# Small remainders of the experts' tokens as segments of one shared tile, in column tiles of TensorE

## The chip, the cores and the metric

The kernel runs on one core of a Trainium2 chip. The metric is the device time of one execution in microseconds (us). The kernel before takes 458.48 us, the median of three runs (458.1 to 458.9).

## The reference: what is computed

An attention block of the RWKV kind gives 3072 rows of 384 numbers; a mixture of eight experts with top-1 routing follows. The attention is not touched by the change and is left out here.

```python
# x: (N, D) = (3072, 384) from the attention; E = 8 experts, F = 1024
logits = x @ w_gate
expert_idx = np.argmax(logits, axis=1)
...                                            # gate_w: the softmax weight of the chosen expert
for e in range(E):
    mask = expert_idx == e
    xe = x[mask]
    h = np.maximum(xe @ w1[e], 0.0)            # (n_e, 384) @ (384, 1024)
    ye = h @ w2[e]                             # (n_e, 1024) @ (1024, 384)
    out[mask] = gate_w[mask, None] * ye
```

The inputs come from a fixed seed, so the number of tokens of each expert is known: 380, 348, 359, 410, 409, 389, 374 and 403. A kernel that works in tiles of 128 tokens of one expert needs 3, 3, 3, 4, 4, 4, 3 and 4 tiles for them, 28 in all. What goes beyond the last multiple of 128 is 124, 92, 103, 26, 25, 5, 118 and 19 tokens: four of the eight remainders are at most 32.

## The kernel before

The first stage (in the trace until about 138 us) is the attention in 32 units, with routing counts beside it; the second is the experts. Each of the 24 groups of 128 rows gets its logits and its expert; VectorE then works out which tile and which row of it each token takes (`ranks`, `bases`, `slots`, `index`), and which expert owns each tile (`owners`). A tile gathers its 128 rows from HBM with an indirect DMA, and scatters its results with another. All data are float32, apart from the one-hot matrices of the routing.

```python
C = 128; NG = N // C                           # 24
NTILE = NG + E - 1                             # 31: the most tiles that routing can need
NSURE = NG + E // 2                            # 28: run in any case
NEARLY = 2                                     # of these, run with tokens of the first half only, early

class Tile:
    def load_w1(self, wp, part=0):             # w1 of the tile's expert, 1536 KB, two buffers
        ...
            e = self.expert(ENG.SP)            # a register, from self.R.ei
            nc.sync.dma_start(self.w1, w1[ds(e, 1)].rearrange("a p d f -> p (a d) f"))

    def turn(self, mo, tag, copy=nc.vector.tensor_copy):
        p = self.R.ps.tile([128, DT, 128], FP32, name="xTp", tag=tag, bufs=BUFS[tag])
        for d in range(DT):                    # DT = 3
            nc.tensor.transpose(p[:, d, :], self.xs[:, 128 * d:128 * d + 128], ident)
        self.xT = self.tile(mo, [128, DT, 128], "xT", 2)
        copy(self.xT, p)

    def hidden(self, mo, fb):                  # fb 0 and 1: half of F each
        ...
        p = self.R.ps.tile([128, 4, 128], FP32, name="hp", tag=f"P{fb}", bufs=2)
        for f in range(4):
            o = (4 * fb + f) * 128
            for d in range(DT):
                nc.tensor.matmul(p[:, f, :], lhsT=self.w1[:, d, o:o + 128], rhs=self.xT[:, d, :],
                                 start=d == 0, stop=d == DT - 1)
        nc.scalar.activation(self.hT[:, 4 * fb:4 * fb + 4, :], p, func=ACT.Relu)

    def result(self, mo):
        p = self.R.ps.tile([128, DM], FP32, name="yp", tag="y", bufs=2)
        e = slice(self.j, self.j + 1) if self.early else ds(self.expert(ENG.PE), 1)
        for f in range(FT):                    # FT = 8; w2 of all experts is resident
            rhs = w2_all[:, e, f * DM:(f + 1) * DM]
            nc.tensor.matmul(p, lhsT=self.hT[:, f, :], rhs=rhs, start=f == 0, stop=f == FT - 1)
        self.y = self.tile(mo, [128, DM], "yo", 3)
        nc.vector.tensor_scalar_mul(self.y, p, self.xs[:, DM:W])

def run_tiles(tiles, wp, mo):                  # called with tiles 2 to 27
    for j, t in enumerate(tiles):
        if j + 2 < len(tiles):
            tiles[j + 2].load_x(mo)
        t.hidden(mo, 0)
        t.hidden(mo, 1)
        if j + 2 < len(tiles):
            tiles[j + 2].load_w1(wp)
        if j + 1 < len(tiles):
            tiles[j + 1].turn(mo, "g")
        t.result(mo)
        t.store()
```

Between the attention and this loop stand two early tiles and the last of the routing (cut to the order of the steps):

```python
t0.hidden(mo, 0); ...                          # routing of the last 6 groups
w2_load(NW); w2_load(NW + 1)                   # 1536 KB each, on SyncE's queue
...
t0.hidden(mo, 1); t1.turn(la, "g", nc.scalar.copy)
R.bases(rt); R.slots(rt); ...; R.owners(rt)    # VectorE
t2.load_w1(wp)                                 # needs owners
t0.result(mo)
R.index(rt, "rw")                              # TensorE and VectorE: the row numbers to gather
t2.load_x(mo); t3.load_x(mo); t0.store()
for e in range(NW + 2, E): w2_load(e)          # the last two
t1.hidden(mo, 0); t1.hidden(mo, 1); t3.load_w1(wp)
t1.result(mo); t1.store(); t2.turn(mo, "g")
late = late_rows(R, NSURE - NEARLY, rt)        # gathers rows for tiles that may not be needed
run_tiles(tiles[2:], wp, mo)
late_tiles(R, NSURE - NEARLY, late)            # under a condition; not taken with these inputs
```

One part of the attention matters for reading the trace: its outputs are written by matmuls that use only half of the array's columns each, so that `hi` = 0 and `hi` = 1 go to different partitions of one PSUM tile.

```python
def u_out(u):
    ...
    yp = ps.tile([128, HC, C], FP32, name="yp", tag="y", bufs=2)
    for c in range(HC):
        ...
        for hi in range(2):
            q = slice(64 * hi, 64 * hi + 64)
            if old is not None:
                nc.tensor.matmul(yp[q, c, :], lhsT=old[:, hi, :], rhs=x["R"][:, c, :],
                                 start=True, stop=False, skip_group_check=True)
        for hi in range(2):
            q = slice(64 * hi, 64 * hi + 64)
            nc.tensor.matmul(yp[q, c, :], lhsT=vh(x, c, hi, 64), rhs=x["A"][:, hi, c, :],
                             start=old is None, stop=True, skip_group_check=True)
```

Of the kernel before, what the change touches and what calls it, by code (L numbers as in the profile page):

```python
# [9 lines left out]
FP32 = mybir.dt.float32  # L10
# [9 lines left out]
E, F = 8, 1024  # L20
# [12 lines left out]
NTILE = NG + E - 1  # L33
NSURE = NG + E // 2
# [12 lines left out]
def rwkv5_then_switch(ctx, tc, r, k, v, rk, tok, wu_in, wl, wg, wgh, w1, w2, out):  # L47

# [345 lines left out]
    def fast():  # L394
# [220 lines left out]
        with tc.manual_schedule():  # L615
# [19 lines left out]
            for u in range(NU):  # L635
                if u + 4 < NU:
                    u_load(u + 4)
                if HP <= u < HP + 4 * NW:
                    w2_load((u - HP) // 4, u % 4, 4)
                elif HP + 4 * NW <= u < HP + 4 * NW + NEARLY * DT:  # L640
                    tiles[(u - HP - 4 * NW) // DT].load_w1(wp, (u - HP - 4 * NW) % DT)
                if u + 2 < NU:
                    u_scale(u + 2)
                    u_scale_g(u + 2)
                if u + 1 < NU:
                    if u:
                        u_scores(u + 1)
                    u_state(u + 1)
                    u_mask(u + 1)
                u_out(u)  # L650
                if u == 2:
                    R.begin()
                    gate_weights()
                if u >= HP and u % HP < HC:
                    u_gate(u // HP - 1, u % HP, "rw")
                for step in todo[u]:
                    step()
                for j in range(NEARLY):
                    if u == NU - HP:
                        tiles[j].load_x(la)  # L660
# [20 lines left out]
            R.bases(rt)  # L681
            R.slots(rt)
# [5 lines left out]
            R.owners(rt)  # L688
            t2.load_w1(wp)
            t0.result(mo)  # L690
            R.index(rt, "rw")
# [5 lines left out]
            t1.hidden(mo, 0)  # L697
# [5 lines left out]
            late = late_rows(R, NSURE - NEARLY, rt)  # L703
            run_tiles(tiles[2:], wp, mo)
        em.close()
        late_tiles(R, NSURE - NEARLY, late)
# [3 lines left out]
    class Routes:  # L710
# [5 lines left out]
        def __init__(self, ps, la, na):  # L716
            self.ps, self.na = ps, na
            self.run = la.tile([128, B + 1, E], FP32, name="run")
            self.rl = la.tile([128, 2, NG], FP32, name="rl")
            self.At = la.tile([128, NG, 128], BF16, name="At")  # L720
            self.la = la
            self.pad = [la.tile([128, E + E // 2], FP32, name=f"pad{i}") for i in range(4)]
            if na:
                self.full = la.tile([128, na], FP32, name="full")
                self.isA = la.tile([128, NG], FP32, name="isA")
# [103 lines left out]
        def bases(self, rt):  # L829

            na = self.na
            ci = rt.tile([128, E], I32, name="ci")
            nc.vector.tensor_scalar_add(ci, self.run[:, B], 127.0)
# [3 lines left out]
            nc.vector.tensor_copy(til[:, z], ci)  # L837
            if na:
                nc.vector.tensor_tensor(til[:, E // 2:E // 2 + na], til[:, E // 2:E // 2 + na], self.full,
                                        op=ALU.subtract)  # L840
            for i in range(3):
                t = self.pad[i + 1]
                nc.vector.tensor_tensor(t[:, z], last[:, z], last[:, E // 2 - (1 << i):E + E // 2 - (1 << i)],
                                        op=ALU.add)
                last = t
            self.last = last[:, z]
            self.base = rt.tile([128, E], FP32, name="base")
            nc.vector.tensor_tensor(self.base, self.last, til[:, z], op=ALU.subtract)
# [3 lines left out]
        def owners(self, rt):  # L852

            tge = rt.tile([1, NTILE, E], FP32, name="tge")
            nc.vector.tensor_tensor(tge, bc(iota_f[0:1, 0:NTILE, None], [1, NTILE, E]),
                                    bc(self.last[0:1, None, :], [1, NTILE, E]), op=ALU.is_ge)
            ef = rt.tile([1, NTILE], FP32, name="ef")
            nc.vector.tensor_reduce(ef, tge, axis=AX, op=ALU.add)
            self.ei = rt.tile([1, NTILE], I32, name="ei")
            nc.vector.tensor_scalar_min(self.ei, ef, float(E - 1))  # L860
            self.nt = rt.tile([1, 1], I32, name="nt")
            nc.vector.tensor_copy(self.nt, self.last[0:1, E - 1:E])

        def slots(self, rt):
# [6 lines left out]
            if self.na:  # L871
                nc.vector.scalar_tensor_tensor(out=jt, in0=self.isA, scalar=-1000.0, in1=jt, op0=ALU.mult, op1=ALU.add)
            Bm = rt.tile([128, NG, NTILE], BF16, name="Bm")
            nc.vector.tensor_tensor(Bm, bc(iota_f[:, None, 0:NTILE], [128, NG, NTILE]),
                                    bc(jt[:, :, None], [128, NG, NTILE]), op=ALU.is_equal)
            self.Bv = rt.tile([128, NG, 2, NTILE], BF16, name="Bv")
            nc.scalar.activation(self.Bv[:, :, 1, :], Bm, func=ACT.Copy, scale=lo_f)
            nc.vector.tensor_tensor(self.Bv[:, :, 0, :], Bm, bc(hi_b[:, :, None], [128, NG, NTILE]), op=ALU.mult)

        def index(self, rt, tag):  # L880
            self.idx = self.to_index(rt, self.Bv, NTILE, NG, tag, "idx")

    class Tile:
# [8 lines left out]
        def load_w1(self, wp, part=0):  # L892
            j, R = self.j, self.R
            if part == 0:
                self.w1 = self.tile(wp, [128, DT, F], "w1s", 2)
            if self.early:
                nc.sync.dma_start(self.w1[:, part], w1[j, :, part])
            else:
                e = self.expert(ENG.SP)
                nc.sync.dma_start(self.w1, w1[ds(e, 1)].rearrange("a p d f -> p (a d) f"))  # L900

        def expert(self, eng):
            return nc.values_load(self.R.ei[0:1, self.j:self.j + 1], engines=[eng], min_val=0, max_val=E - 1,
# [24 lines left out]
        def hidden(self, mo, fb):  # L928
# [5 lines left out]
            for f in range(4):  # L934
                o = (4 * fb + f) * 128
                for d in range(DT):
                    nc.tensor.matmul(p[:, f, :], lhsT=self.w1[:, d, o:o + 128], rhs=self.xT[:, d, :],  # L937
# [19 lines left out]
    def run_tiles(tiles, wp, mo):  # L957

        for j, t in enumerate(tiles):
            if j + 2 < len(tiles):  # L960
                tiles[j + 2].load_x(mo)
            t.hidden(mo, 0)
            t.hidden(mo, 1)
            if j + 2 < len(tiles):
                tiles[j + 2].load_w1(wp)
            if j + 1 < len(tiles):
                tiles[j + 1].turn(mo, "g")
            t.result(mo)
            t.store()

    def late_rows(R, first, pool):

        xs = pool.tile([128, NTILE - first, W], FP32, name="xl")
        late = [Tile(R, j, late=True) for j in range(first, NTILE)]
        for i, t in enumerate(late):
            t.load_x(xs[:, i])
        return late

    def late_tiles(R, first, tiles):

        count = nc.values_load(R.nt[0:1, 0:1], min_val=0, max_val=NTILE,
                               skip_runtime_bounds_check_because="at most NTILE tiles by their count")
        with tc.If(count > first):
            with tc.tile_pool(name="lt", bufs=1) as lt:
                with tc.manual_schedule():
                    for t in tiles:
                        t.load_w1(lt)
                        t.turn(lt, "g")
                        t.hidden(lt, 0)
                        t.hidden(lt, 1)  # L990
# [3 lines left out]
    def after_general():  # L994
# [10 lines left out]
        R.owners(rt)  # L1005
# [3 lines left out]
        with tc.manual_schedule():  # L1009
# [4 lines left out]
            late = late_rows(R, NSURE, rt)  # L1014
            run_tiles(tiles, mo, mo)
        em.close()
        late_tiles(R, NSURE, late)
# [15 lines left out]
def _layout(name, *a):  # L1033
# [26 lines left out]
    elif name == 'moe_w1':  # L1060
        a = a.reshape(E, DT, 128, F).transpose(0, 2, 1, 3)
# [24 lines left out]
```

## Time and profile before

| what | value |
|---|---|
| time, median of 3 runs | 458.48 us |
| span of the profiled execution | 456.2 us |
| TensorE matmul, busy | 439.0 us (96% of the span) |
| TensorE weight load, busy | 368.0 us (81%) |
| VectorE, ScalarE, GpSimd, busy | 147.1, 129.2, 158.2 us |
| moved by DMA | 95.45 MB, mean 209 GB/s |
| w1 loads of a tile in the loop | 26, 1536 KB each, 6.7 us to landing |

Busy times are sums of the records of an engine; records of one engine overlap on TensorE, because its matmuls are pipelined, so the start-to-start distance of its records tells more than their length. A float32 matmul of this program leaves two records: 48 of them are the 24 matmuls of one tile's two `hidden` calls, 16 are the eight of its `result`. In the rows of the chain of waits, the first number is the start of a step, the second its length, both in us. In the timeline, a row is one group of like instructions that follow one another: start, length, engine, line, operation, tiles, shapes, count. An array use is given as rows*columns (128*64 is half the columns).

### The profile page before, as it was taken

The page shows a single profiled execution, that of the slowest core. Times are in us where ns is not written, and L with a number is a line of the kernel's source. Part 1 is how long each engine was busy: PE and PEld are TensorE (multiplying, and loading weights), DVE is VectorE, ACT ScalarE, POOL GpSimd, SP SyncE. Part 2 cuts the span into 40 slices and gives each one's busy share as a digit, 9 for nine tenths or more (in the row PEclk, how much of TensorE's full clock was granted, in tenths as well). Part 3 has the DMA queues.
Part 4 walks back from the last instruction along what each step waited for, and adds up shares of the span by engine and source line. Part 5 has one row for each costly group of instructions (what it writes and reads, how often), then busy time and mean ns, then how long its engine had stood idle before and what let it go on. Part 6 is the DMA issues. An engine that isn't in the chain of part 4 may idle for free.

```text
span 456.2 us, 10424 instructions
## 1 busy us (share of the span) xinstructions
PE 439.0 (96%) x4176; PEld 368.0 (81%) x4176; DVE 147.1 (32%) x394; ACT 129.2 (28%) x390; POOL 158.2 (35%) x192
## 2 busy tenths in 40 slices
PE   7899998998999988999999999999999999999993
PEld 7799997997999876887777777778888888888871
DVE  6576785996896401111111111111111111111100
ACT  3777775775773101111111111111111111111110
POOL 6997747946840243111111111111122221111000
PEclk9999998998999999999999999999999999999999
DMA  7488859869743999644555555555544544555400
GB/s 274 127 262 287 301 163 374 337 194 376 301 140 118 394 415 285 243 172 169 185 181 191 190 199 190 175 192 177 174 159 174 180 167 175 180 183 174 157 19 13
DMA packets 24576, 95.45 MB, mean 209 GB/s; under 512 B 3840, under 2 KB 6950, under 8 KB 20676
## 3 DMA queue, kind: packets, MB, share of 16 engines
q1 hardware_dynamic: 20322, 83.40, 51.2%
q0 software_dynamic: 3904, 11.23, 8.3%
q8 instruction: 38, 0.62, 0.5%
q14 instruction: 22, 0.18, 0.1%
q10 hardware_dynamic: 290, 0.02, 0.0%
HBM read 85.18 MB, written 10.24 MB: 209 GB/s over the span
## 4 chain that ended last, share of the span: by engine, by line
PE 51%; issue 36%; POOL 6%; DMA 2%; another core or an unknown queue 1%; DVE 1%; ACT 1%; POOLq 0%; SPq 0%; ACTq 0%; DVEq 0%
PE hp L937 13%; PE yp L946 12%; PE P L497 5%; PE yp L558 5%; PE P L487 5%; PE yp L554 4%; PE rp L587 4%; POOL xs L918 3%; PE Gp L533 2%; DMA w_all<-in_r_k_units_dram 2%; POOL out_dram L951 2%; PE xTp L924 1%; PE warm L444 1%; POOL w_all L467 0%
## 5 line engine op out<-in xcount | busy, mean ns | idle before, releaser
L937 PEld LDWEIGHTS hp<-xT,w1s 128*128 128x128 f32 x1344 | 154.3, 192 | 7.8 <-DVE xT L926 1.1
L937 PE MATMUL hp<-xT,w1s 128*128 128x128 f32 x1344 | 155.1, 275 | 0.8 <-DVE xT L926 0.8
L946 PE MATMUL yp<-w_all,hT 128*128 (+1 forms) x448 | 149.5, 487 | 1.6 <-ACT hT L939 1.2
L946 PEld LDWEIGHTS yp<-w_all,hT 128*128 128x128 f32 x448 | 82.9, 190 | 54.1 <-ACT hT L939 1.8
L939 ACT ACTIVATE hT<-hp 128x512 f32<-128x512 f32 x56 | 33.4, 597 | 265.5 <-PE hp L937 252.3
L951 POOL DMA_INDIRECT out_dram<-yo,idx x26 | 26.5, 1018 | 221.7 <-DVE yo L948 212.2
L508 ACT ACTIVATE A<-ident,dv 128x128 f32<-128x128 f32 x192 | 59.6, 389 | 0.2 <-ACT dv L505 0.2
L926 DVE COPY xT<-xTp 128x384 f32<-128x384 f32 x27 | 15.1, 557 | 132.2 <-PE xTp L924 122.4
L948 DVE TENSOR_SCALAR yo<-yp,xs 128x384 f32<-128x384 f32 x26 | 16.1, 618 | 123.4 <-PE yp L946 123.4
L466 POOL TENSOR_TENSOR w_all<-w_all 128x384 f32<-128x384 f32 x31 | 34.8, 1123 | 27.2 <-DMA w_all<-in_r_k_units_dram 9.9
L558 PE MATMUL yp<-A,w_all 128*64 128x128 f32 x384 | 40.5, 282 | 0.1
L519 DVE COPY_PREDICATED A<-mask,P 128x384 f32<-128x384 int32 x64 | 33.8, 583 | 9.6 <-ACT A L508 9.4
L918 POOL DMA_INDIRECT xs<-x_hbm,idx x26 | 25.3, 974 | 29.8 <-PE hp L937 22.5
L554 PE MATMUL yp<-w_all,St 128*64 128x128 f32 x320 | 33.5, 282 | 0.0
L467 POOL TENSOR_TENSOR w_all<-w_all,W 128x384 f32<-128x384 f32 x31 | 33.2, 1071 | 0.0
L497 PE MATMUL P<-w_all 48*128 48x128 f32 x384 | 30.0, 289 | 0.8 <-DVE w_all L468 0.5
L487 PEld LDWEIGHTS P<-wu,w_all 48*128 48x128 f32 x384 | 24.0, 187 | 7.4 <-POOL w_all L466 3.9
L487 PE MATMUL P<-wu,w_all 48*128 48x1 f32 x384 | 26.5, 249 | 3.4 <-POOL w_all L466 3.4
L558 PEld LDWEIGHTS yp<-A,w_all 128*64 128x64 f32 x384 | 26.6, 142 | 0.9 <-DVE A L519 0.5
L468 DVE TENSOR_TENSOR w_all<-w_all,W 128x384 f32<-128x384 f32 x32 | 25.3, 794 | 5.6 <-DMA w_all<-in_r_k_units_dram 4.8
L497 PEld LDWEIGHTS P<-w_all 48*128 48x128 f32 x384 | 24.5, 191 | 1.2 <-issue 0.7
L475 POOL TENSOR_TENSOR w_all<-w_all,Wg 128x288 f32<-128x288 f32 (+1 forms) x32 | 24.3, 759 | 2.4 <-ACT dv L505 2.0
(133 smaller groups left out, 265.2 us busy)
## 6 DMA issues: line engine op xcount, KB each, us to landing
w1s<-in_moe_w_dram SPq DMA_DIRECT2D x26, 1536.0 KB, 6.7
w_all<-in_r_k_units_dram SPq DMA_DIRECT2D x32, 384.0 KB, 6.3
w_all<-in_v_k_units_dram SPq DMA_DIRECT2D x32, 288.0 KB, 4.9
w_all<-in_moe_w_dram SPq DMA_DIRECT2D x16, 384.0 KB, 5.4
w_all<-in_moe_w_dram SPq DMA_DIRECT2D x4, 1536.0 KB
w1s<-in_moe_w_dram SPq DMA_DIRECT2D x6, 512.0 KB, 8.7
x_hbm<-w_all SPq DMA_DIRECT2D x4, 577.5 KB, 6.4
x_hbm<-xb SPq DMA_DIRECT2D x4, 577.5 KB, 4.6
```

The costliest lines, as they stand in the source:

```text
L466: nc.gpsimd.tensor_tensor(x["RK"], x["r"], x["k"], op=ALU.mult)
L487: nc.tensor.matmul(P[hi][:, o:o + 1], lhsT=x["RK"][q, c, :], rhs=wu[q, 1, hp:hp + 1], start=True, stop=True, skip_group_check=True)
L497: nc.tensor.matmul(P[hi][:, c * C:(c + 1) * C], lhsT=x["K"][q, c, :], rhs=x["R"][q, c, :], start=True, stop=True, skip_group_check=True)
L508: nc.scalar.activation(A[:, hi, c, :], ident, func=ACT.Copy, scale=dv[:, hi, c:c + 1])
L519: nc.vector.copy_predicated(A[:, hi], bc(mask[:, None, :].bitcast(I32), [128, HC, C]), P[hi][:, 0:HC * C].rearrange("p (c t) -> p c t", t=C))
L554: nc.tensor.matmul(yp[q, c, :], lhsT=old[:, hi, :], rhs=x["R"][:, c, :], start=True, stop=False, skip_group_check=True)
L558: nc.tensor.matmul(yp[q, c, :], lhsT=vh(x, c, hi, 64), rhs=x["A"][:, hi, c, :], start=old is None, stop=True, skip_group_check=True)
L918: nc.gpsimd.indirect_dma_start(out=self.xs, out_offset=None, in_=x_hbm[:, :], in_offset=off)
L937: nc.tensor.matmul(p[:, f, :], lhsT=self.w1[:, d, o:o + 128], rhs=self.xT[:, d, :], start=d == 0, stop=d == DT - 1)
L939: nc.scalar.activation(self.hT[:, 4 * fb:4 * fb + 4, :], p, func=ACT.Relu)
L946: nc.tensor.matmul(p, lhsT=self.hT[:, f, :], rhs=rhs, start=f == 0, stop=f == FT - 1)
L951: s_ = nc.gpsimd.indirect_dma_start(out=out[:, :], out_offset=bass.IndirectOffsetOnAxis(ap=self.idx, axis=0), in_=self.y[:, :], in_offset= ...
```

## The change

Remainders of at most 32 tokens no longer get a tile of their own. Up to four of them share one tile: its partitions 0 to 31 belong to the first expert, 32 to 63 to the second, and so on. 24 full tiles are run in any case, and this one; more full tiles, or a second shared tile, are run under the condition at the end, which these inputs do not meet.

The shared tile works with tokens as the stationary operand: for each of four quarters of F, and for each of three blocks of D, four matmuls of 32 columns each (one for each expert) write 32 partitions of one PSUM tile. `quarter` gives a quarter of the hidden layer, `turn_quarter` transposes it, `add` multiplies it by a quarter of w2 of each expert. The four w1 quarters and the four w2 quarters are loaded for all four experts, eight loads of 4 x 384 KB. The parts are put between the two halves of `hidden` of every second tile, and two such loads are kept in flight. For this, w1 lies in HBM in quarters of F, and the routing puts the segments' columns behind the tiles' columns.

```diff
-NTILE = NG + E - 1
-NSURE = NG + E // 2
+SEG = 32
+NS = 4
+NTILE = (N + E * (C - 1 - SEG)) // C
+NCOL = NTILE + E
+NSURE = NG
+FQ = 4
+FW = F // FQ
...
             R.bases(rt)
+            R.order(rt)
             R.slots(rt)
...
-            R.owners(rt)
+            R.owners(rt, NSURE - NEARLY)
             t2.load_w1(wp)
             t0.result(mo)
+            t1.hidden(mo, 0)
             R.index(rt, "rw")
             t2.load_x(mo)
             t3.load_x(mo)
             t0.store()
             for e in range(NW + 2, E):
                 w2_load(e)
-            t1.hidden(mo, 0)
             t1.hidden(mo, 1)
...
-            late = late_rows(R, NSURE - NEARLY, rt)
-            run_tiles(tiles[2:], wp, mo)
+            late = late_rows(R, NSURE - NEARLY, [xbs[1][:, i] for i in range(G)] + [t0.xs, t1.xs])
+            run_tiles(tiles[2:], wp, mo, Segments(R, 0))
...
+        def order(self, rt):                  # VectorE: which column belongs to which segment
+            self.seg = rt.tile([128, E], FP32, name="seg")
+            nc.vector.tensor_tensor(self.seg, self.til[:, 0], self.til[:, 1], op=ALU.subtract)
+            self.tge = rt.tile([128, NTILE, E], FP32, name="tge")
+            nc.vector.tensor_tensor(self.tge, ..., op=ALU.is_ge)
+            tsg = rt.tile([128, NTILE, E], FP32, name="tsg")
+            nc.vector.tensor_tensor(tsg, self.tge, ..., op=ALU.mult)
+            ...                               # reduce, add; segs; own (twice); sp; reduce; add
...
         def index(self, rt, tag):
-            self.idx = self.to_index(rt, self.Bv, NTILE, NG, tag, "idx")
+            self.idx = self.to_index(rt, self.Bv, NCOL, NG, tag, "idx")
+            self.idxs = rt.tile([128, E // NS], I32, name="idxs")
+            for i in range(E):
+                q = slice(SEG * (i % NS), SEG * (i % NS) + SEG)
+                nc.scalar.copy(self.idxs[q, i // NS:i // NS + 1], self.idx[0:SEG, NTILE + i:NTILE + i + 1])
...
+    class Segments(Tile):
+        def load(self, mo, i):
+            q = i % FQ
+            ...
+            self.w[i] = self.tile(mo, [128, NS, DT * FW], "wq", 2)
+            for k, e in enumerate(self.es):
+                src = ...                     # quarter q of w1[e], or of w2[e]
+                nc.sync.dma_start(self.w[i][:, k], src)
+        ...
+        def quarter(self, mo, q):
+            p = self.R.ps.tile([128, FW], FP32, name="hg", tag="rw", bufs=1)
+            for d in range(DT):
+                for i in range(NS):
+                    t = slice(SEG * i, SEG * i + SEG)
+                    nc.tensor.matmul(p[t, :], lhsT=self.xT[:, d, t], rhs=self.w[q][:, i, d * FW:(d + 1) * FW],
+                                     start=d == 0, stop=d == DT - 1, skip_group_check=True)
+            self.h = mo.tile([128, FW], FP32, name="hk", bufs=1)
+            nc.scalar.activation(self.h, p, func=ACT.Relu)
+
+        def turn_quarter(self, q):            # two transposes, and a copy by VectorE
+            ...
+        def add(self, q):
+            if q == 0:
+                self.p = self.R.ps.tile([128, DM], FP32, name="yg", tag="rw", bufs=1)
+            n = FT // FQ
+            for f in range(n):
+                for i in range(NS):
+                    t = slice(SEG * i, SEG * i + SEG)
+                    nc.tensor.matmul(self.p[t, :], lhsT=self.hT[:, n * q + f, t],
+                                     rhs=self.w[FQ + q][:, i, f * DM:(f + 1) * DM], ...)
...
     def run_tiles(tiles, wp, mo, seg):
         for j, t in enumerate(tiles):
+            i = (j - 5) // 2 if j % 2 and 5 <= j < 5 + 4 * FQ else None
             ...
             t.hidden(mo, 0)
+            if i is not None:
+                if i < FQ:
+                    seg.quarter(mo, i)
+                else:
+                    seg.add(i - FQ)
+                if i + 2 < 2 * FQ:
+                    seg.load(mo, i + 2)
             t.hidden(mo, 1)
+            if i is not None and i < FQ:
+                seg.turn_quarter(i)
             if j + 2 < len(tiles):
                 tiles[j + 2].load_w1(wp)
+            if j in (2, 3):
+                seg.load(mo, j - 2)
             if j + 1 < len(tiles):
                 tiles[j + 1].turn(mo, "g")
+            if j == 4:
+                seg.turn(mo, "rw")
             t.result(mo)
             t.store()
+            if i == 2 * FQ - 1:
+                seg.result(mo)
+                seg.store()
```

The rows gathered ahead for tiles that may not be needed become eight (seven tiles and a second shared one), from five; the two early tiles' w1 comes in four parts each, from three.

## The prediction

> **What bounds the kernel now.** I read three views in this order: busy time by stage, the chain that ended last, and the timeline of TensorE. The first cuts the span where the stages change (columns: busy us and number of records of each engine, then granted clock, DMA share and GB/s):
>
> ```profile
> 0.00:11.00 11.00, 8.64 (x64) 8.47 (x65) 7.47 (x32) 3.92 (x10) 7.95 (x30) 1.00 0.78 271
> 11.00:134.00 123.00, 118.07 (x2097) 108.77 (x2097) 93.77 (x251) 85.69 (x309) 91.64 (x103) 0.97 0.79 267
> 134.00:178.00 44.00, 41.53 (x356) 33.36 (x353) 16.50 (x63) 9.77 (x23) 9.70 (x10) 1.00 0.78 280
> 178.00:438.00 260.00, 260.00 (x1607) 209.16 (x1606) 28.11 (x48) 28.67 (x48) 46.91 (x47) 1.00 0.52 181
> ```
>
> From 178 to 438 us TensorE is busy for 260.00 of 260.00 us, at a clock of 1.00, while no other engine passes 47 us. That alone doesn't say that its work is dense, since its records overlap. The chain does:
>
> ```profile
> 177.85 5.36 PE hp L937 x48
> 183.54 5.16 PE yp L946 x16
> 188.70 5.36 PE hp L937 x48
> 194.39 5.16 PE yp L946 x16
> 199.55 5.36 PE hp L937 x48
> ```
>
> From one `hp` to the next is 199.55 - 188.70 = 10.85 us: 5.36 for 48 records of the hidden layer, 5.16 for 16 of the result, and 0.33 left for three transposes, 0.11 each. Nothing waits. A record of 128 moving columns costs 5.36 / 48 = 0.112 us, one of 384 columns 5.16 / 16 = 0.322 us; halfway between, 256 columns should cost 0.217 us. 24 tiles of 10.85 us are 260 us, so the loop is bound by TensorE's columns and by nothing else. A tile costs this whether it has 128 tokens or 5. The later rows of the same chain show GpSimd's gathers and "issue"; I don't follow them, since TensorE has no gap there.
>
> The timeline shows what the change relies on, column tiles:
>
> ```profile
> 126.37 0.39 PE L554 MATMUL yp<-w_all,St 128*64 128x128 f32 x4
> 126.59 0.39 PE L558 MATMUL yp<-A,w_all 128*64 128x128 f32 x4
> 126.81 0.39 PE L554 MATMUL yp<-w_all,St 128*64 128x128 f32 x4
> 127.03 0.39 PE L558 MATMUL yp<-A,w_all 128*64 128x128 f32 x4
> ```
>
> Groups of four records of 128 columns start 0.22 us apart, 0.055 us a record, against 0.112 on the whole array: two tiles of 64 columns run side by side at full rate, with different stationary operands, and in L558 different moving operands too.
>
> **What the Trainium skill says.** "TensorEngine Tiling (Array Packing)", Key Properties: tiles run loads and matmuls independently, and a change of the tiling mode drains TensorE. The trace agrees on the first (the groups above). For the second it gives a size:
>
> ```profile
> 138.55 2.29 PE rp L587 x48
> 140.84 2.87 PE hp L937 x24
> ```
>
> 48 records of L587 on half the columns take 2.29 us where three groups of 16 take 0.71 each elsewhere in the chain (2.13), and the 24 full-array records after them 2.87 instead of half of 5.36 (2.68): some 0.16 and 0.19 us at the two ends, so I allow 0.33 us a visit. "TensorE: Matmul & The Clock Gate", Part 3, gives 2.38x for three column tiles and 3.07x for four row tiles, measured as single bursts. No four-column tile occurs before, so that factor is taken beyond what this trace shows. The same part says that matmuls start strictly in order. The timeline disagrees:
>
> ```profile
> 60.12 0.34 PE L587 MATMUL rp<-IW,y 128*64 128x104 f32 x2
> 60.22 0.27 PE L558 MATMUL yp<-A,w_all 128*64 128x128 f32 x1
> ```
>
> The last L558 record of this unit starts at 60.22 us, after two of L587, which the program has behind it and which use the other half of the columns. So I expect one stream not to hold up the others. This matters, because the two records of a matmul use the same column tile: were starts strictly in order, each would hold up the next tile, and only two of four would ever overlap.
>
> **The change part by part.**
>
> Removed: the counts of the inputs give 28 tiles before, all of them run, and 24 after, since the four remainders 26, 25, 5 and 19 become segments; they fill one shared tile, and the conditional part stays untaken. 4 x 10.85 = **43.4 us** less of the loop. With each tile go 1.57 MB of w1, a gather and a scatter, all hidden before.
>
> Added on TensorE, in its own order of work, thus all on the path:
> - four quarters: 12 matmuls, 24 records of 256 columns. Spread over four streams, 6 x 0.217 = 1.30 us each; 5.2 in all.
> - four adds: 8 matmuls, 16 records of 384 columns, 4 x 0.322 = 1.29 us each; 5.2 in all.
> - eight visits to the other tiling mode: 8 x 0.33 = 2.6.
> - transposes: 3 for the rows and 4 x 2 for the quarters, 11 x 0.11 = 1.2.
>
> Sum **14.2 us**. ScalarE's relu and VectorE's copies for it lie behind at least half a `hidden` (2.68 us) before they are needed; both engines are busy for some 28 of 260 us.
>
> Added on the DMA: eight loads of 1.57 MB, less four w1 loads: +6.3 MB. Two tiles and one load move 2 x (1.57 + 0.4) + 1.57 = 5.5 MB in 2 x 10.85 + 2 = 23.7 us, 232 GB/s; the stage had 181, and 134 to 178 us had 280. A load goes out four tiles before its use (43 us), the next w1 two tiles before, against 6.7 us to landing. Hidden.
>
> Added ahead of the loop on VectorE, where the index depends on it. Sizes from like rows of 144 to 154 us: five operations of 8 to 37 elements at 0.17 us (one in `bases`, four in `order`) 0.85; three of 232 elements at 0.40 (the old 248-element `tge` took 0.40) 1.2; four of 64 at 0.21, 0.84; `Bm` and `Bv` 888 instead of 744 elements, 0.93 and 0.94 us scaled, together 0.36; in `owners` two of 64 elements before `ei`, 0.4. That is **3.7 us** later for `ei` (152.6 before) and the index (153.9). `hidden(mo, 0)` of the second early tile, put ahead of the index, fills TensorE for 2.68 us of it. What remains is the DMA queue: t2's w1 went out at 153.3 us, with the queue full from 148 to 174 us (about 0.77 MB in 2 us). Going out at 157 instead, it leaves the queue empty for 1 to 2 us, once the two w2 loads of 144 and 145 us are through; the later w2 and w1 loads land as much later. TensorE meets that at t2's result: before, it already waited there for w2 until 171.0. I take **+2 us**, an estimate, 0 to 5 possible. The three more gathers at 1.3 us each on GpSimd end near 176 us and t4's rows are needed at 183: hidden.
>
> 458.5 - 43.4 + 14.2 + 2.0 = **431.3 us**.
>
> **The rivals.**
>
> *Only two column tiles overlap.* The quarters and adds cost 4 x 2.60 + 4 x 2.58 = 20.7 instead of 10.4 us: 441.6. For it: in-order starts as the skill states, and two is all that this trace shows. Against: the drifting streams. I give it, and worse, 15%.
>
> *No overlap at all* (four moving streams too many for the operand reads): 41 us of matmuls eat the gain whole, 462. Against it: two different streams already run at full rate. 3%.
>
> *A middle rate,* three of four as in the skill's row-tile figure, or a dearer mode change (0.6 us a visit): +3 us, 434. 25%.
>
> *The loads become the bound*: if w1 waited behind the segment's 1.57 MB. Both together, 3.1 MB at 280 GB/s, take 11 us and have over 16. Weak, and would show as TensorE waiting for a DMA before `hp` in every second tile.
>
> *The start costs more*: if t2's w1 lands after t1's result (about 164 us) TensorE waits outright; up to +5 us. Equally the waits around t2 of before (yp's second half came only at 175.0) could shrink: -2 us.
>
> **Range and chances.** The centre is 431.5. The low end, 427, is cheap mode changes (0.15 us a visit, -1.4), and a start that loses nothing (-2), with a little besides. The high end, 439, takes the middle rate and a bad start together; it leaves out the two-stream case, whose weight with the tails is the 2 in 10. To stay within 2% the time must be over 449.3, which only missing overlap reaches: 4%; slower needs more than that besides: 1%.
>
> **What the profile after would show.** A loop period still 10.85 us in even tiles, and in odd tiles of the right range about 1.6 us more (1.9 with the transposes). `hp` has 24 x 48 = 1152 records instead of 1344. 96 records of 256 columns and 64 of 384 in 128*32 form, starting in groups of four some 0.22 and 0.32 us apart; groups of two would be the first rival, singles the second. TensorE still without gaps in the loop, DMA near 230 GB/s in its middle. The loop's first tile beginning some 2 us later than 164.65. If the start moves by more than 5 us, or the odd tiles wait for w1, the prediction is wrong by that.

## The result, and the profile after

The changed kernel takes 439.67 us (median of four runs, 437.61 to 441.83), against 458.69 us of the kernel before: a ratio of 0.9588, with a 95% interval of 0.954 to 0.9635. That is 19 us faster where 27 were predicted, and just outside the range that ended at 439; the four runs, 437.61 to 441.83, lie on both sides of that edge. The profiled execution is the longest of the four: its span is 440.0 us, against 456.2 before.

The busy time by stage first (columns as in the prediction):

```profile
220.00:400.00 180.00, 180.00 (x1205) 140.11 (x1204) 20.04 (x36) 20.06 (x35) 31.99 (x32) 1.00 0.64 227
```

Inside the loop nothing is wrong: TensorE has no gap in these 180 us, the clock is 1.00, and the DMA moves 227 GB/s (232 was worked out). The chain that ended last shows the shared tile's visits, with quarters (`hg`) first and adds (`yg`) later:

```profile
231.40 2.68 PE hp L981 x24
234.08 1.43 PE hg L1036 x24
235.51 2.88 PE hp L981 x24
...
244.10 5.36 PE hp L981 x48
...
325.57 2.68 PE hp L981 x24
328.25 1.43 PE yg L1056 x16
329.67 2.87 PE hp L981 x24
...
338.04 5.36 PE hp L981 x48
```

A tile with a quarter takes 244.10 - 231.40 = 12.70 us and one with an add 338.04 - 325.57 = 12.47, that is 1.85 and 1.62 more than the 10.85 of a plain tile. 4 x 1.85 + 4 x 1.62, and 0.33 for the transposes of the shared rows, are 14.2 us.

The loss stands elsewhere. The timeline of TensorE ahead of the loop and in its first tiles (the bracket gives the idle time before a group, and what ended it):

```profile
167.13 0.72 PE L968 MATMUL xTp<-ident,xs 128*128 128x128 f32 x3 [2.48 <-DMA xs<-x_hbm,idx]
168.50 8.30 PE L981 MATMUL hp<-xT,w1s 128*128 128x128 f32 x48 [0.65 <-DVE xT L970]
...
183.03 5.52 PE L981 MATMUL hp<-xT,w1s 128*128 128x128 f32 x48
191.12 0.81 PE L968 MATMUL xTp<-ident,xs 128*128 128x128 f32 x3 [2.57 <-DMA xs<-x_hbm,idx]
191.73 6.81 PE L990 MATMUL yp<-w_all,hT 128*128 x16
198.37 5.52 PE L981 MATMUL hp<-xT,w1s 128*128 128x128 f32 x48
```

TensorE waits twice for gathered rows (`xs`), and each time the work after it is slow: 48 `hp` records take 8.30 us instead of 5.52, 16 `yp` records 6.81 instead of 5.33. The windows of this stretch give the reason for the slowness in the clock's column, and one for the waits in the last two:

```profile
158.00:178.00 20.00, 16.88 (x88) 13.64 (x87) 1.67 (x6) 2.71 (x10) 12.56 (x13) 0.83 0.99 373
178.00:188.00 10.00, 9.37 (x59) 7.29 (x58) 1.18 (x2) 1.20 (x2) 2.00 (x2) 1.00 0.79 121
188.00:198.00 10.00, 7.43 (x23) 4.52 (x23) 0.56 (x1) 0.60 (x1) 0.00 (x0) 0.83 0.90 377
```

Around both waits the granted clock falls to 0.83 on average. From 178 to 188 us the DMA engines move almost nothing but gathered rows, and reach 121 GB/s with it.

Before, TensorE came through the same stretch without a wait of more than 1.2 us, and at a clock of 1.00:

```profile
164.65 5.62 PE L937 MATMUL hp<-xT,w1s 128*128 128x128 f32 x48 [0.85 <-DVE xT L926]
...
183.05 0.49 PE L924 MATMUL xTp<-ident,xs 128*128 128x128 f32 x3
...
188.54 5.52 PE L937 MATMUL hp<-xT,w1s 128*128 128x128 f32 x48
```

Cut at two marks, the two spans compare like this (the third tile of the loop is t4 of the prediction, the first t2):

| stretch of the profile | before, us | after, us | difference |
|---|---|---|---|
| start to the `hp` of the third tile of the loop | 188.54 | 198.37 | +9.83 |
| from there to the last `yp` record | 259.69 | 230.50 | -29.19 |
| from there to the end | 7.98 | 11.13 | +3.15 |
| span | 456.21 | 440.00 | -16.21 |

The middle row is 43.4 - 14.2 = 29.2 us, to the first decimal what was predicted. The first row was predicted at +2, and the last at 0. Of the first row, 1.07 us come from the attention, which ends that much later in the profile after (TensorE's first transposes behind it start at 139.07 us instead of 138.00). The experiments are about these two rows.

### The profile page after: what moved, and what is told of

It reads as the page before. It is cut to its first block, busy times and chain, and to the rows that moved or that the text cites. A ratio compares the mean times of both kernels' runs of the same rounds, so it can differ in the third digit from the quotient of the medians.

```text
span 440.0 us, 10264 instructions
## 1 busy us (share of the span) xinstructions
PE 415.4 (94%) x4079; PEld 343.6 (78%) x4079; DVE 149.5 (34%) x407; ACT 127.5 (29%) x394; POOL 155.6 (35%) x189
## 4 chain that ended last, share of the span: by engine, by line
PE 81%; DMA 7%; POOL 3%; issue 3%; DVE 2%; ACT 1%; POOLq 0%; SPq 0%
PE hp L981 27%; PE yp L990 26%; PE P L503 5%; PE yp L564 4%; DMA w_all<-in_r_k_units_dram 4%; PE P L493 4%; DMA xs<-x_hbm,idx 3%; PE yp L560 3%; PE rp L593 3%; PE Gp L539 2%; PE xTp L968 2%; PE warm L110 2%; PE hg L1036 1%; PE yg L1056 1%; POOL xb L962 1%
## 5 line engine op out<-in xcount | busy, mean ns | idle before, releaser
L981 PEld LDWEIGHTS hp<-xT,w1s 128*128 128x128 f32 x1152 | 135.7, 195 | 11.2 <-issue 4.1
L981 PE MATMUL hp<-xT,w1s 128*128 128x128 f32 x1152 | 138.0, 279 | 0.6 <-DVE xT L970 0.6
L990 PE MATMUL yp<-w_all,hT 128*128 (+1 forms) x384 | 129.6, 491 | 0.6 <-ACT hT L983 0.6
L990 PEld LDWEIGHTS yp<-w_all,hT 128*128 128x128 f32 x384 | 71.8, 192 | 46.3 <-ACT hT L983 1.2
L983 ACT ACTIVATE hT<-hp 128x512 f32<-128x512 f32 x48 | 28.7, 597 | 238.0 <-PE hp L981 216.3
L995 POOL DMA_INDIRECT out_dram<-yo,idx x22 | 22.4, 1019 | 204.0 <-DVE yo L992 194.5
L992 DVE TENSOR_SCALAR yo<-yp,xs 128x384 f32<-128x384 f32 x22 | 13.6, 618 | 106.2 <-PE yp L990 106.2
L970 DVE COPY xT<-xTp 128x384 f32<-128x384 f32 x23 | 12.8, 556 | 104.6 <-PE xTp L968 93.3
L962 POOL DMA_INDIRECT xs<-x_hbm,idx x22 | 21.5, 976 | 31.6 <-PE hp L981 25.5
L564 PEld LDWEIGHTS yp<-A,w_all 128*64 128x64 f32 x384 | 28.3, 142 | 0.9 <-DVE A L525 0.5
```

Of the source, the lines that this page charges most:

```text
L962: nc.gpsimd.indirect_dma_start(out=self.xs, out_offset=None, in_=x_hbm[:, :], in_offset=off)
L981: nc.tensor.matmul(p[:, f, :], lhsT=self.w1[:, q, d, o:o + 128], rhs=self.xT[:, d, :], start=d == 0, stop=d == DT - 1)
```

## The experiments

The theory in them: the loop is as predicted, and the loss has three parts: the queue of gathers ahead of the loop (eight late ones instead of five), the longer routing ahead of the first gather, and the end of the program. The rivals: the segment's loads slow the loop; the weights' loads alone delay the rows; each wait adds its own loss; a larger skipped block costs a longer jump.

**The shared tile left out.** The 24 full tiles remain; the output lacks 75 tokens.

```diff
-            run_tiles(tiles[2:], wp, mo, Segments(R, 0))
+            run_tiles(tiles[2:], wp, mo, None)      # and every step of seg under "if seg"
```

> The changed kernel without the shared tile: its gather, its 32 weight loads, its quarters, adds and scatter are left out (75 tokens are not written); the 24 full tiles, the longer routing and the start stay. Column tiles as counted (four side by side, theory 1): the loop loses the 14.2 us that the trace adds up to, so about 425.5 us from 439.7. If the segment's 12.6 MB of loads also slow other tiles (theory 2), it falls by more than 15 us. The stretch before the loop's third tile should not change: its wait for rows at 188 to 191 us has nothing to do with the segment.

Measured: 422.93 us (the median of three; a fourth execution, 429.37 us, was in a slower state and is left out), ratio 0.9203 (0.9171 to 0.9236). From the third tile's `hp` (194.07) to the last `yp` record (410.37) it takes 216.30 us, 14.2 less than the 230.50 of the changed kernel: this is the segment's whole cost in the loop, its 12.6 MB of loads included. The time fell by 16.7, more than expected; the rest lies ahead of the loop. There the profiles differ from run to run: TensorE's first transposes after the attention start at 137.59 us here and at 139.07 in the changed kernel. Over all profiles of this study that start varies from 136.9 to 139.5, with no order by kernel, so differences of 1 to 2 us between two kernels are not read as more than that here. The wait for the third tile's rows varies too: 2.57 us in the changed kernel and 1.14 here, though the code is the same up to there. The 14.2 us count against the loads as a rival.

**Seven late items.** The second shared tile is left out of the conditional part, so more than four small remainders would not be covered.

```diff
-        late += [Segments(R, j, late=True) for j in range(1, E // NS)]     # in the usual path only
```

> The changed kernel with seven instead of eight late items: the second shared tile, which these inputs never need, is left out of the conditional part, with its gather. Theory 1 (the tail): skipping the conditional part waits for the last eight scatters' semaphores if it holds eight scatters, so for the very last one; with seven it does not. The distance from the start of the last scatter to the end falls from 9.5 to 6.5 us. Rival (a longer jump over a larger block): it stays near 9 us. At the start one gather fewer is queued ahead of the third tile's: its wait shrinks by up to 1.9 us. Together 3 to 6 us faster than the changed kernel: 434 to 437 us.

Measured: 434.65 us, ratio 0.946 (0.9438 to 0.9481). The line of the conditional, asked for by itself, shows what GpSimd's sequencer does at the end (min/median/max ns, then first and last start in us); first the changed kernel:

```profile
L1111 POOLq EVENT_SEMAPHORE  x4: 17/43/3563, 430.7 to 430.9; - x4
L1111 POOLq COMPARE_BRANCH  x2: 38/46/53, 430.5 to 435.1; - x2
```

and the one with seven items:

```profile
L1111 POOLq EVENT_SEMAPHORE  x3: 43/43/43, 425.3 to 425.4; - x3
L1111 POOLq COMPARE_BRANCH  x2: 38/46/53, 425.1 to 426.1; - x2
```

With eight scatters in the part that is skipped, GpSimd waits 3.56 us before its second branch, 435.1 - 430.5 = 4.6 us after the first; with seven it waits for nothing and needs 1.0. The last scatter was issued just before, at 430.29, and the last of its packets starts at 434.0. So the skip waits for the very last scatter, and the way to the end comes after that instead of beside it. From the start of the last scatter to the end it is 9.71 us after, 6.23 with seven items, 6.56 before (five items). The jump itself isn't longer.

The start gained as well, and more than expected: with one gather fewer, TensorE turns the third tile's rows at 187.13 us without the wait of 2.57, and the tile's `hp` starts at 192.94, 5.4 us earlier than in the changed kernel's profile, where a wait shorter by up to 1.9 us was expected. So this run's 5 us are both causes together; only the end of the program isolates the skip.

**The late gathers spread in the loop.** All eight items stay.

```diff
-            late = late_rows(R, NSURE - NEARLY, [...])          # eight gathers here
+            late = late_rows(R, NSURE - NEARLY, [...], load=False)
...                                                              # in run_tiles:
+            if 6 <= j < 6 + len(rows):
+                rows[j - 6].load_x(rows[j - 6].rows)
```

> The changed kernel with the eight late gathers one at a time in the loop's tiles 6 to 13 instead of all ahead of the loop. Theory 1 (queue of gathers): the third loop tile's rows, which came 14 us after their issue, come in time, so the 2.6 us wait of TensorE at 188 us and the half clock after it (1.5 us) go: about 4 us, 435.5 us. Rival (the rows are late because the weights fill the DMA engines): the wait stays and so does the time. The tail stays at 9.5 us, as eight items remain in the conditional part.

Measured: 436.01 us, ratio 0.9481 (0.9456 to 0.9505). TensorE's timeline:

```profile
167.60 0.52 PE L968 MATMUL xTp<-ident,xs 128*128 128x128 f32 x3 [2.63 <-DMA xs<-x_hbm,idx]
168.77 8.55 PE L981 MATMUL hp<-xT,w1s 128*128 128x128 f32 x48 [0.65 <-DVE xT L970]
...
188.00 0.49 PE L968 MATMUL xTp<-ident,xs 128*128 128x128 f32 x3
...
193.49 2.73 PE L981 MATMUL hp<-xT,w1s 128*128 128x128 f32 x23
```

The second wait is gone and its half clock too: the third tile's `hp` starts at 193.49 instead of 198.37. GpSimd issued this tile's gather at 167.2 us, behind no late gather, where it was 177.0 before. The first wait is as it was; its rows were asked for ahead of the late gathers, so it has another cause. The end stays at 9.8 us, as expected with eight items.

One pair of profiles could mislead here, so the stretch is also counted from TensorE's first transposes after the attention: the third tile's `hp` starts 54.1 us after them with the gathers spread and 54.3 with seven items, but 59.3 in the changed kernel and 61.7, 60.3 and 56.5 in the three other profiles whose code is the same up to there (the changed kernel again, the loops exchanged, the shared tile left out). All four are longer, by at least 2.1 us.

**A busy TensorE in the first wait.**

```diff
             t1.store()
+            idle(11)                     # 22 records of a 128x128 dummy product
             t2.turn(mo, "g")
```

> The changed kernel with 11 dummy matmuls (about 2.5 us) in TensorE's wait ahead of the first loop tile, so that it stays busy. The clock should stay at 1.00 there and the first tile's 48 hidden records take 5.5 instead of 8.3 us. Theory 1 (the gathers' queue sets the end of the start): the time stays within 1 us of the changed kernel, because the third tile's rows land at 191 us all the same and its wait grows by what is saved. Rival (each wait adds its own loss): 2.5 to 3 us faster, 437.

Measured: 438.43 us, ratio 0.9535 (0.951 to 0.956): 1.2 us under the changed kernel's first measurement, with overlapping intervals. The 48 `hp` records of the first tile take 5.62 us instead of 8.30, so it was the idle time that had brought the clock down, and 2.7 us are won there. In the profile most of it lasts: the third tile's `hp` starts at 196.05 us instead of 198.37. But the rest of the loss only changed its place: the third tile's rows were there in time at 190.56, and TensorE stood 2.97 us in the first tile's `yp` instead, with a slow group after it (4.41 us for 8 records instead of 2.85). Neither expectation is confirmed by the 1.2 us. What held it is not shown by the profile ("remote"); its end, at 180.3 us, lies close to that of the weights' loads in the trace. A wait was replaced by another, so the waits of one profile can't simply be added up.

**The changed kernel again**, beside the next three.

> The changed kernel as it is, once more, beside the others of this chip: 437 to 442 us as before. Two details are looked at again: the wait of the third loop tile for its rows (near 191 us) and 9.5 us or so from the start of the last scatter to the end.

Measured: 442.37 us, ratio 0.9659 (0.9633 to 0.9686); third tile's `hp` at 198.71, 9.87 us from the last scatter to the end.

**Late items alone, in the kernel before.**

```diff
-            late = late_rows(R, NSURE - NEARLY, rt)
+            late = late_rows(R, NSURE - NEARLY, rt, 3)          # three more gathers and bodies
```

> The kernel before with eight instead of five late tiles (three gathers more ahead of the loop, three bodies more in the conditional part, which is not taken). Theory: 3 us more from the last scatter to the end (9.5 instead of 6.5), as the skip now waits for the last scatter itself; the third loop tile's rows come up to 5.7 us later (three gathers of about 1.9 us), against a slack of some 5 us, so 0 to 3 us there. Together 461.5 to 465. Rival (the late items cost nothing, the longer routing does all): 458.5 to 459.5.

Measured: 468.72 us, ratio 1.0236 (1.0205 to 1.0267): 11.3 us slower, far more than expected. TensorE:

```profile
187.52 0.87 PE L924 MATMUL xTp<-ident,xs 128*128 128x128 f32 x3 [6.94 <-DMA xs<-x_hbm,idx]
188.19 7.54 PE L946 MATMUL yp<-w_all,hT 128*128 x16
195.56 5.52 PE L937 MATMUL hp<-xT,w1s 128*128 128x128 f32 x48
```

The third tile's gather went out at 174.71 and its rows came 12.8 us later. The loop starts 195.56 - 188.54 = 7.0 us late, 2.2 of it half clock (7.54 against 5.33), and the end takes 10.29 instead of 6.56 us. The size was missed: up to 3 us had been allowed for the start, and the slack of some 5 us in the expectation was not there. This run alone carries the two causes that the changed kernel's late items have, without any shared tile.

**The longer routing alone, in the kernel before.** The added operations' results are not used.

```diff
             R.bases(rt)
+            R.order(rt)                  # twelve operations of the shapes of the change
             R.slots(rt)                  # with 37 columns
...
             t0.result(mo)
+            t1.hidden(mo, 0)             # moved up, as in the change
             R.index(rt, "rw")            # and eight ScalarE copies
```

> The kernel before with the routing work of the changed one alone: twelve more VectorE operations of the same shapes ahead of the slots, 37 instead of 31 columns, eight small ScalarE copies after the index, and the second early tile's first half ahead of the index; the results of the added operations are not used, and tiles and late items stay as before. Theory: the first loop tile's gather goes out near 159 instead of 154.8 us, TensorE waits for its rows (over 2 us) and falls to half clock (2.7 us), so the loop begins about 5 us later: 463 to 464 us. If the order of work hides it, as the prediction had it: 460 to 461.

Measured: 460.86 us, ratio 1.0066 (1.0032 to 1.01). The number falls into the second range, but the kernel before took 457.45 beside it, and 3.4 us more is between the two expectations, which had been made from 458.5. TensorE waits 2.27 us for the first tile's rows and falls to half clock after it (7.25 us for the `hp`), as in the changed kernel, and the third tile's `hp` starts at 193.06, 4.5 us late. The end is 6.61 us, as with five items it should be.

**A shorter way to the first tile**, on top of the spread gathers.

```diff
-            nc.vector.tensor_tensor(rb, ...)                    # and the product for Bv
+            nc.gpsimd.tensor_tensor(rb, ...)
...
-            R.owners(rt, NSURE - NEARLY)
-            t2.load_w1(wp)
+            w2_load(NW + 2)
             t0.result(mo)
             t1.hidden(mo, 0)
             R.index(rt, "rw")
+            R.owners(rt, NSURE - NEARLY)
+            t2.load_w1(wp)
...
-            for e in range(NW + 2, E):
-                w2_load(e)
+            w2_load(NW + 3)
```

> The changed kernel with the late gathers spread in the loop as before (436.0 us), and in addition a shorter way to the first loop tile: two products of the routing on GpSimd instead of VectorE (0.35 and 1.09 us of VectorE), the index ahead of the owners (1.1 us), and one of the two last w2 loads ahead of the owners, so that the queue of loads has no gap. If the index path sets the first tile's wait, its gather goes out near 157 instead of 159.5 us, the wait of 2.6 us shrinks below 1, the clock stays up, and the time falls to 431 to 433. If the loads set it (bytes through the queue), it stays within 1 us of 436.

Measured: 432.35 us, ratio 0.9455 (0.9419 to 0.9491), against 442.37 us of the changed kernel beside it. It computes all that the changed kernel does and is the fastest version here that does. TensorE:

```profile
163.27 0.52 PE L971 MATMUL xTp<-ident,xs 128*128 128x128 f32 x3 [0.36 <-DMA xs<-x_hbm,idx]
166.85 5.60 PE L984 MATMUL hp<-xT,w1s 128*128 128x128 f32 x48 [3.06 <-DMA w1s<-in_moe_w_dram]
172.28 0.49 PE L971 MATMUL xTp<-ident,xs 128*128 128x128 f32 x3
...
188.62 3.62 PE L984 MATMUL hp<-xT,w1s 128*128 128x128 f32 x31
```

The wait for rows shrinks to 0.36 us, and a wait for w1 takes its place, 3.06 us; but the clock stays, and the third tile starts at 188.62, where the kernel before had it (188.54). That the clock stays after 3.06 us is in part luck, as a run below shows: with the same code up to there, it fell after 2.54.

**The same, with both w2 loads back behind the owners.**

> The same as the run with the shorter way (a_start, 432.35 us), but with both last w2 loads where the change has them, behind the owners and the first loop tile's w1. If the index path (two products on GpSimd, index ahead of the owners) brings the gain, it stays within 1 us of 432.4. If the unbroken queue of loads brings part of it, the w1 loads land later and TensorE waits for w1 or w2 near 165 to 178 us: 433.5 to 436.

Measured: 437.72 us, ratio 0.9553 (0.9527 to 0.958), beyond the upper end expected. The wait for rows is gone here too, yet TensorE waits 2.23 us for w1 and then 2.12 us ahead of `yp`, each time with a slow group after it (7.22 us for 48 `hp`, 7.09 for 16 `yp`), and the third tile starts at 194.42. The spread gathers alone had 436.01 and a ratio of 0.9481 against 0.9553 here, so the faster index by itself gains nothing and rather loses: it removes the wait for rows, but w1, which now goes out behind the index, comes too late. The place of one w2 load is all that differs from the run before, and 5.4 us lie between the two medians (4.5 by the ratios, as the two ran on different chips). Of this, 3.4 us are the two slow groups, which that run was spared. The start is as much a matter of bytes as of the index.

**Both, and seven late items.**

> The spread gathers and the shorter way to the first loop tile (432.35 us beside a changed kernel of 442.37), and seven late items instead of eight: the second shared tile is left out of the conditional part, so that more than four small remainders would not be covered; these inputs have four. If the tail is the skip's wait for the last scatter, 3.2 to 3.6 us less: 428.5 to 429.5 us, with 6.2 to 6.6 us from the last scatter to the end. If the eight items mattered only through their gathers, already spread, it stays at 432.

Measured: 430.95 us, ratio 0.9399 (0.9377 to 0.942); the end takes 6.28 us. The end is shortened as expected; the time lies 1.5 us above the expectation. In its profile the attention ends 1.4 us later than in the one without this step (138.76 against 137.32), and the clock falls in the wait for w1, which that one got over at full clock:

```profile
167.66 7.22 PE L984 MATMUL hp<-xT,w1s 128*128 128x128 f32 x48 [2.54 <-DMA w1s<-in_moe_w_dram]
```

These are 7.22 - 5.60 = 1.6 us more, after a shorter wait (2.54 us against 3.06).

**The shared tile's loops exchanged**, so that one expert's matmuls follow one another.

```diff
-            for d in range(DT):
-                for i in range(NS):
+            for i in range(NS):
+                for d in range(DT):      # and likewise in add
```

> The changed kernel with the loops of the quarters and adds exchanged: the matmuls of one expert, which use the same column tile, follow one another in the program (six records in a quarter, four in an add) before the next expert's. If starts are strictly in the program's order, the tiles can overlap only at the seams: a quarter takes some 4 us instead of 1.43 and the whole 15 to 20 us more. If each column tile runs its own stream ahead, a quarter stays near 1.5 us and the time at the changed kernel's 437 to 442.

Measured: 448.3 us in one run. The chain:

```profile
235.51 2.80 PE hg L1036 x24
238.31 2.88 PE hp L981 x24
...
335.13 1.45 PE yg L1056 x16
336.58 2.88 PE hp L981 x24
```

Neither expectation holds. With four records of 384 columns in a row on one column tile (`yg`) nothing is lost; with six of 256 (`hg`), a quarter takes 2.80 instead of 1.43 us. So the column tiles do run ahead of one another, but only so far.

## Why the prediction was right and wrong

**Right: what the loop loses and gains.** 43.4 us less and 14.2 more were predicted, and 29.19 net is what the two profiles differ by. The step taken beyond the trace, four column tiles side by side, held: 24 records of 256 columns and the change of mode in 1.43 us, where one after the other they would take 24 x 0.217 = 5.2. "TensorEngine Tiling (Array Packing)", Key Properties, agrees with these runs: tiles run independently, and the change of mode has a price, here 1.43 - 1.30 = 0.13 us going in and 2.88 - 2.68 = 0.20 coming out, together the 0.33 that was allowed. That the price is the drain which the page names is not shown; the runs show its size.

**Right: the loads of the loop.** 227 GB/s, no wait for w1 in the loop, and a loop that shrinks by 14.2 us, no more, when the segment's loads are left out.

**Wrong: "the three more gathers at 1.3 us each on GpSimd end near 176 us and t4's rows are needed at 183: hidden".** GpSimd did end there; the third tile's gather went out right behind:

```profile
176.99 0.95 POOL L962 DMA_INDIRECT xs<-x_hbm,idx  x1 [0.31 <-DMA xb<-x_hbm,idx]
```

The step that failed is counting what issuing a gather costs and not what the queue behind it needs. Before, the gathers of the loop's tiles land 3.1 us after their issue (median); at that pace this one would have been there at 180. With 197 KB each (128 rows of 1540 bytes), at the 121 GB/s seen while almost nothing else ran, a gather takes some 1.6 us by estimate, more than the 1.25 us that GpSimd needs from one issue to the next; so they pile up, and the ones ahead of the third tile's made it land 14 us after its issue. The sign stood in the profile before: its five late gathers took 9.3 us to landing (median). Spreading them gave 4.9 us of start back, one fewer 5.4, and eight items in the kernel before cost 7.0.

**Wrong in size: "+2 us" for the routing.** The parts were right: 3.7 us of VectorE work were counted, and in the profile the index comes 158.37 - 153.70 = 4.7 us later, 1.1 of it from an attention that ended later. Even the start of the first tile's `hp` is not far off, 168.50 - 164.65 = 3.85 us with these 1.1. What failed is that the wait of 2.5 us was not followed further: the clock fell in it, and 8.30 instead of 5.52 us for the next `hp` is more than the wait itself. The routing alone cost 3.4 us in the kernel before. The wait until 171.0 us that the prediction puts down to w2 is 0.41 us long in the timeline, and no load is named for it there.

**Missing: the end.** No step looked at the conditional part, because these inputs skip it. With eight scatters in it the skip itself waits for the last scatter: +3.15 us, and 3.5 us back with seven.

Of the prediction's five rivals three were about the column tiles and one about the loop's loads. The one that came true, a dearer start, did so by size and not by cause: it expected t2's w1 to be late, and TensorE waited for gathered rows. It had been limited to 5 us, since only the first tile was looked at in it. The sum of what was missed, 7.8 us in the start and 3.15 at the end, is the 11 us between the two spans' difference (16.21) and the 27.2 predicted; by the medians 8.2 us are missing.

The two causes in the start don't add up. Counted from the attention's end, the third tile starts 8.8 us later with the change, 8.1 with the late items alone and 3.9 with the routing alone. With the late items alone TensorE stands 6.94 us before the third tile's rows, and in the changed kernel, where it comes to them later, 2.57.

Not settled: why the third tile's rows are waited for between 1.14 and 5.93 us in four profiles with the same code up to there; what held the first tile's `yp` in the run with dummy matmuls until 180.3 us; and how much each of the two steps in the shorter way would give without the other; only one of the two was run.

## What to carry to other kernels

A burst of work that "costs only its issue" on a side engine fills the queue behind it: look at when the last of its transfers lands, and keep what may never be needed away from the moment at which the loop starts. Where TensorE is the bound, a wait of 2 to 3 us is to be counted with the slower clock that can follow it, 1.6 to 3 us more for the next 48 records here. And a part that is never executed has a price at the place where it is skipped: count the transfers in it.

## What the runs showed of the hardware

- The last of several gathers landed 12.8, 14 and 15 us after its issue, with eight late ones ahead of it (late items alone, the changed kernel, and again); with almost nothing beside them gathers moved 121 GB/s while the engines' busy share was 0.79.
- A gap of some 2.5 us in TensorE's work, with one of 0.65 soon after, was followed by half clock for 6.8 us in the profile's clock record (from 167.3 us), and 22 dummy records in it prevented that. "TensorE: Matmul & The Clock Gate", Why this matters for your kernels, asks for no gap over about 3 us; these runs show that less can be enough, 2.23 us where w1 came late, and that 3.06 us in another run left the clock up. The length of a gap alone does not decide.
- Column tiles take their work from the program's order with a limited look-ahead: up to four records in a row on one tile left all four tiles busy, six in a row lengthened a quarter from 1.43 to 2.80 us. The strict order of starts that Part 3 of the same page states does not hold here: in the exchanged loops the second expert's first record starts 0.46 us after the first expert's first (235.90 and 235.44 us in the trace), with three of the first expert's six still to start. In the adds of that run the four experts' first records start within 0.04 us (335.06 to 335.10), each with three of the expert before still to start. Both would fit three records waiting on each column tile; other numbers were not tried.
